# The second norm's features by 32x32 block transposes on VectorE and a round trip through memory

## The chip, the cores and the metric

One core of a Trainium2 chip runs the whole program. The metric is the device time of one execution in microseconds, as a median over runs. TensorE (PE in the profile) multiplies matrices and can transpose through the multiplier; PEld is its loading of stationary operands. VectorE is DVE, ScalarE is ACT, GpSimd is POOL, and SyncE (SP) here only issues transfers (DMAs).

## The reference

A transformer block with adaptive norms: attention on a modulated layer norm of `x`, then a gated MLP with a mixing over positions on a second modulated layer norm.

```python
x = A_x                                                     # 1 x 2048 x 448, float32
sa, ca, ga, sb, cb, gb = (silu(c) @ w_mod) in six parts of 448
h = layernorm(x) * (1 + ca) + sa
x = x + ga * attention(h, A_wqkv, A_wo)                     # 16 heads of 28
h = layernorm(x) * (1 + cb) + sb                            # the second norm
z = gelu(h @ B_w_in)                                        # 2048 x 1792
z1, z2 = z[..., :896], layernorm(z[..., 896:])
g = B_w_sp @ z2 + B_b_sp[:, None]                           # mixes the 2048 positions
out = x + gb * ((z1 * g) @ B_w_out)
```

## The kernel before

Everything is float32. Where precision matters, an operand is split in a high part (rounded to the matmul's reduced float32) and a low part, the difference, and a product is 11 matmuls over pairs of parts (`STEPS`): blocks 0 to 2 of the split hold the high parts of 384 features, blocks 3 to 5 their low parts, and block 6 the high and low parts of the last 64 features in its two halves. There is no scheduler: each engine's order is that in which the code is written (`manual_schedule`), and semaphores are put in where data or buffers demand it. One queue of SP carries nearly all transfers; a transfer that must wait holds up those behind it.

The stages in order: first norm and q, k, v; attention, head by head; then, from about 868 us, the part that this document is on; from 977 us the z2 product and its norm, the mixing over positions (a scheme with fewer products, given by tables), and the output product.

The 2048 rows are 16 tiles of 128, in four groups of four. In the part in question:

- `wo_mm(t)` is the output projection of attention for tile t, 11 matmuls into one PSUM bank; `wo_add(t)` adds it on DVE to the rows `x3[t]` and stores the sum to `x2_scr` for the end of the kernel. The last two matmuls of tiles 0 to 7 (`STEPS_Z`) wait for the last head and for `o_split`.
- `h2_stats(g)` takes mean and variance of a group's four tiles on DVE and 1/sqrt by a power on GpSimd (`rstd_of`). `h2_norm(g)` normalises the rows in place by two DVE instructions a tile: 448 columns, and the last 64 again beside them (they are wanted twice, for the halves of block 6).
- `h2_group(g)` calls `ln_transpose`: 16 TensorE transposes of 128x128 with the identity into four PSUM banks `tp`, so that features lie on partitions and 512 rows of the group along the free dimension. Then, for each of the four blocks, ACT applies scale and shift by feature into `hfull`, ACT copies that to the high part in `h2T[g]`, and DVE subtracts for the low part.
- `z1_unit(g, f)`, 28 of them, multiplies 128 columns of `w_in` with `h2T[g]` (11 matmuls), takes the gelu on ACT and stores the result to `z1_scr`. PSUM has seven banks in rotation here, so unit n reuses the bank of unit n - 7, once its gelu has read it.

`h2_group(0)` and `(1)` stand among the last projection tiles, `(2)` and `(3)` among the z1 units. The rows of `x` come in four loads, in which a group's row 128 t + p lies on partition p of tile t. `x2_load` at the end reads tile t back for the last addition. Buffers are reused by tags: `heapE` and `heapC` hold the `h2T` of groups 2 and 3, `x3` has three slots for the rows of groups 0 to 2 (group 3 lies in `heapC`) and later holds the buffer of the gelu outputs.

Of the kernel before, what the change touches and what calls it, by code (L numbers as in the profile page):

```python
# [8 lines left out]
F32 = mybir.dt.float32  # L9
F32R = mybir.dt.float32r  # L10
# [10 lines left out]
NG = 4  # L21
# [78 lines left out]
def tile_adaln_mha_gmlp(ctx, tc, x, wqkv, wo, w_in, w_spT, b_sp, w_out, cT, w_mod0, w_mod, out):  # L100
# [11 lines left out]
    x2_scr = scr.tile([S, D], F32, name="x2_scr")  # L112
    z1_scr = scr.tile([FH, S], F32, name="z1_scr")
    ws_scr = scr.tile([4 * len(W_SUMS), 128, 512], F32, name="ws_scr")
    wo2_scr = scr.tile([2, 7, 128, D], F32, name="wo2_scr")
    wl_scr = scr.tile([2 * len(W_SUMS), 128, 512], F32, name="wl_scr")

# [16 lines left out]
    def hview(heap, off, a, b):  # L134
        return heap[:, off : off + a * b].rearrange("p (a b) -> p a b", b=b)
# [913 lines left out]

    def h2_norm(g):  # L1050
        mv, rs, _ = mv3.pop(g)
        for tt in range(4):
            xt = x3[4 * g + tt]
            for o, i in ((xt[:, D:], xt[:, 384:D]), (xt[:, :D], xt[:, :D])):
                dve.tensor_scalar(
                    out=o, in0=i, scalar1=mv[:, tt, 0:1], scalar2=rs[:, tt : tt + 1], op0=ALU.subtract, op1=ALU.mult
                )

    raw_in = {}

# [53 lines left out]
        wo_mm(t, STEPS_MAIN)  # L1114
    o_split(3, 0, dve)
    o_split(3, 1, dve)
    for t in range(4):
        wo_mm(t, STEPS_Z)
        wo_add(t)
    o_split(3, 2, dve)  # L1120
    for t in range(4, 8):
        wo_mm(t, STEPS_Z)
        wo_add(t)
    o_split(3, 3, dve)
    h2_stats(0)
    h2_stats(1)
    h2_norm(0)
    heapF = dpool.tile([128, 4 * 896], F32R, name="heapF", tag="heapF")
    w2 = Halves(4, hview(heapD[2], 0, 4, 896), hview(heapF, 0, 4, 896))
    stg.close()  # L1130
    t3b = ph3.enter_context(tc.tile_pool(name="t3b", bufs=2))

    heaps = []

    def h2_group(g, after=None):
        if g >= 2:
            heaps.append(fh.tile([128, 4 * 896], F32R, name="heap", tag=("heapE", "heapC")[g - 2]))
            h2T.append(hview(heaps[-1], 0, 7, 512))
        xns = [x3.pop(4 * g + t) for t in range(4)]
        ln_transpose(xns, t3b, h2T[g], cols["cb"], cols["sb"], (act,) * 4, (dve,) * 4, None, after)  # L1140

    zbuf = []

# [18 lines left out]
    def last_tile(c):  # L1162
        if c == 2:
            wo_tile(15)
        h2_stats(2, ((0, 2, 1, 3).index(c),))

    h2_group(1, last_tile)
    h2_norm(2)
    h2_stats(3)
    win_load(0, t3)  # L1170
    win_load(1, t3b)
# [443 lines left out]
```

## Time and profile before

| | |
|---|---|
| median of 3 runs | 1377.51 us (1377.08 to 1378.38) |
| span of the profiled execution, first to last instruction | 1376.2 us |
| median less that span | 1.3 us |
| granted TensorE clock in the profile | 1.000 |
| stretch from the last attention sums to the z2 product | 868.3 to 977.1 us |
| TensorE transposes of the second norm | 64, from 892.6 to 932.1 us |

The profile lists the profiled execution's span and no other time of it; what lies around the span is therefore given by the difference to the median. The page gives each engine's busy time and share, the chain of work that ended last (followed back from the last instruction to whatever released each step), and groups of instructions by source line. The timeline gives instructions in order, runs of equal ones merged, with the engine's idle time before them and what ended it. A matmul's recorded duration contains its pipeline, so the cost of a run of matmuls is read from start to start.

### The profile page before, as it was taken

The page shows a single profiled execution, that of the slowest core. Times are in us where ns is not written, and L with a number is a line of the kernel's source. Part 1 is how long each engine was busy: PE and PEld are TensorE (multiplying, and loading weights), DVE is VectorE, ACT ScalarE, POOL GpSimd, SP SyncE. Part 2 cuts the span into 40 slices and gives each one's busy share as a digit, 9 for nine tenths or more (in the row PEclk, how much of TensorE's full clock was granted, in tenths as well). Part 3 has the DMA queues.
Part 4 walks back from the last instruction along what each step waited for, and adds up shares of the span by engine and source line. Part 5 has one row for each costly group of instructions (what it writes and reads, how often), then busy time and mean ns, then how long its engine had stood idle before and what let it go on. Part 6 is the DMA issues. An engine that isn't in the chain of part 4 may idle for free.

```text
span 1376.2 us, 20532 instructions
## 1 busy us (share of the span) xinstructions
PE 1370.9 (100%) x7098; PEld 974.6 (71%) x7098; DVE 1067.5 (78%) x1688; ACT 805.1 (59%) x1472; POOL 359.9 (26%) x367
## 2 busy tenths in 40 slices
PE   9999999999999999999999999999999999999998
PEld 8888655555555555555555554888898888888898
DVE  7898888888888888888888880673367777999752
ACT  6623666676667666766677779464324544555420
POOL 2134335243624264645640002200011000000000
PEclk9999999999999999999999999999999999999999
DMA  8465757777667667777773110535604665788552
GB/s 292 138 172 180 226 143 228 201 220 206 230 197 229 188 226 238 231 207 232 231 218 101 37 44 23 174 142 190 216 16 152 223 202 187 248 281 269 181 174 98
DMA packets 137075, 254.28 MB, mean 185 GB/s; under 512 B 21832, under 2 KB 37322, under 8 KB 134426
## 3 DMA queue, kind: packets, MB, share of 16 engines
q1 hardware_dynamic: 134254, 248.79, 57.7%
q10 hardware_dynamic: 2718, 4.19, 0.9%
q8 instruction: 56, 0.92, 0.3%
q14 instruction: 47, 0.39, 0.1%
HBM read 174.53 MB, written 73.59 MB: 180 GB/s over the span
## 4 chain that ended last, share of the span: by engine, by line
PE 97%; DVE 2%; issue 0%; DMA 0%; ACTq 0%; ACT 0%; POOL 0%; DVEq 0%
PE st_ps L741 19%; PE o_ps L756 17%; PE mt L709 17%; PE z_ps L1373 5%; PE acc L1441 5%; PE acc L1442 5%; PE acc L1440 5%; PE pq L404 5%; PE z_ps L1147 5%; PE pv L386 2%; PE y_ps L1508 2%; PE y_ps L1509 2%; PE y_ps L1507 2%; PE acc L1449 1%; PE acc L1450 1%; PE acc L1448 1%
## 5 line engine op out<-in xcount | busy, mean ns | idle before, releaser
L714 DVE TENSOR_REDUCE pm<-mt 128x1 f32<-128x512 f32 x1024 | 630.6, 680 | 86.1 <-PE mt L709 86.1
L745 ACT ACTIVATE P<-st_ps 128x512 f32<-128x512 f32 x1024 | 515.4, 626 | 202.6 <-PE st_ps L741 201.8
L741 PE MATMUL st_ps<-qst,kst 128*128 128x512 f32 x1024 | 406.3, 406 | 0.0
L709 PE MATMUL mt<-kst,qst 128*128 128x512 f32 x1024 | 402.8, 393 | 0.0
L741 PEld LDWEIGHTS st_ps<-qst,kst 128*128 128x128 f32 x1024 | 191.6, 188 | 140.8 <-issue 93.0
L756 PE MATMUL o_ps<-P,V 128*32 128x512 f32 x2048 | 246.3, 599 | 0.0
L709 PEld LDWEIGHTS mt<-kst,qst 128*128 128x128 f32 x1024 | 192.7, 188 | 31.5
L869 POOL TENSOR_TENSOR ws_raw<-ws_raw 128x512 f32<-128x512 f32 x112 | 143.6, 1288 | 177.7 <-DMA ws_raw<-in_w_spT_dram 110.5
L1357 ACT ACTIVATE heapB<-raw_sp 128x512 fp32r<-128x512 f32 x156 | 96.7, 630 | 98.4 <-PE acc L1442 68.3
L756 PEld LDWEIGHTS o_ps<-P,V 128*32 128x32 f32 x2048 | 53.7, 109 | 122.8 <-issue 117.4
L1442 PE MATMUL acc<-heapB,heapA 128*128 128x512 f32 x312 | 121.5, 390 | 0.0
L1440 PE MATMUL acc<-heapB,heapA 128*128 128x512 f32 x312 | 121.5, 390 | 0.0
L150 DVE TENSOR_TENSOR heapB<-raw_sp,heapB 128x512 fp32r<-128x512 f32 x112 | 74.6, 686 | 28.0 <-ACT heapB L1357 27.8
L1441 PE MATMUL acc<-heapB,heapA 128*128 128x512 f32 x222 | 86.6, 390 | 0.0
L1440 PEld LDWEIGHTS acc<-heapB,heapA 128*128 128x128 f32 x312 | 58.6, 188 | 12.2
L1442 PEld LDWEIGHTS acc<-heapB,heapA 128*128 128x128 f32 x312 | 58.6, 188 | 12.0
L404 PE MATMUL pq<-heapD,heapD 128*128 128x512 f32 x196 | 61.9, 390 | 0.0
L150 POOL TENSOR_TENSOR ws_raw<-ws_raw 128x512 fp32r<-128x512 f32 x44 | 56.6, 1287 | 3.5
L785 POOL TENSOR_TENSOR osb<-osb,rb 128x512 f32<-128x512 f32 x15 | 19.2, 1280 | 112.0 <-DMA rb<-r_scr 93.3
L1441 PEld LDWEIGHTS acc<-heapB,heapA 128*128 128x128 f32 x222 | 41.7, 188 | 8.9 <-DVE heapB L150 0.3
L1376 ACT ACTIVATE z<-z_ps 128x448 f32<-128x448 f32 x32 | 17.4, 544 | 47.7 <-PE z_ps L1373 47.7
L170 POOL TENSOR_TENSOR rsz<-rsz,mhalf 128x1 f32<-128x1 f32 x16 | 14.3, 891 | 118.1 <-DVE rsz L169 118.1
(218 smaller groups left out, 1652.8 us busy)
## 6 DMA issues: line engine op xcount, KB each, us to landing
ws_raw<-in_w_spT_dram SPq DMA_DIRECT2D x136, 256.0 KB
ws_scr<-ws_raw SPq DMA_DIRECT2D x112, 256.0 KB
ws_raw<-ws_scr SPq DMA_DIRECT2D x88, 256.0 KB
raw_sp<-ws_scr SPq DMA_DIRECT2D x88, 256.0 KB
raw_sp<-in_w_spT_dram SPq DMA_DIRECT2D x68, 256.0 KB
wl_scr<-ws_raw SPq DMA_DIRECT2D x44, 256.0 KB
kst<-qk_scr SPq DMA_DIRECT2D x45, 224.0 KB
qst<-qk_scr SPq DMA_DIRECT2D x45, 224.0 KB
```

The lines of the kernel that those rows point to most:

```text
L150: eng.tensor_tensor(out=dst, in0=a, in1=hi.bitcast(F32), op=ALU.subtract)
L404: pe.matmul(pq, wqk[:, b, m * 128 : (m + 1) * 128], hT[g][:, a, :], start=j == 0, stop=j == NST - 1)
L709: pe.matmul(mt, qst[h % 3][:, t * 128 : (t + 1) * 128], kst[h % 3][:, kb * 512 : (kb + 1) * 512], start=True, stop=True)
L714: dve.tensor_reduce(out=pms[h][:, t, kb : kb + 1], in_=mt, axis=AX.X, op=ALU.max)
L741: pe.matmul(st, kst[h % 3][:, kt * 128 : (kt + 1) * 128], qst[h % 3][:, qb * 512 : (qb + 1) * 512], start=True, stop=True)
L745: act.activation(p, st, AF.Exp, scale=SCALE)
L756: pe.matmul(otile[h][32 * qb : 32 * qb + 32, :], V[:, kt, h, :], ptiles.pop((u, qb)), start=kt == 0, stop=kt == NT - 1)
L869: pool.tensor_tensor(out=a, in0=a, in1=b, op=ALU.add if W_SUMS[v][2] > 0 else ALU.subtract)
L1357: act.activation(hi, raw[0], AF.Copy)
L1440: pe.matmul(o, zh[:, c], hi, start=p < 2 and kt == 0, stop=False, skip_group_check=p > 1)
L1441: pe.matmul(o, zh[:, c], lo, start=False, stop=False, skip_group_check=p > 1)
L1442: pe.matmul(o, zl[:, c], hi, start=False, stop=kt == 3, skip_group_check=p > 1)
```

## The change

The transposes of the second norm leave TensorE. The rows of a group are now normalised by ACT (one instruction a tile, with the scale 1/std and a bias `nb` = -mean/std that DVE computes in one small instruction). `h2_turn` lets DVE transpose all 32x32 blocks of a 128x448 tile in one instruction, four tiles a group, into a buffer `turn`, and four transfers store it, 32 partitions each, to `hs_scr[g]` in memory with features as rows. `h2_load` brings it back in five transfers into the low-part blocks of `h2T[g]` and both halves of block 6. `h2_group` then applies scale and shift from there on ACT, copies to the high parts, and subtracts into the low parts on DVE.

Block transposes leave the 32-row groups where they are, so the rows of `x` are laid out in another order when they are handed in: partition 32 a + i of tile t holds row 128 a + 32 t + i of its group. The program up to the second norm works on rows in that order unchanged; the stores put them in the true order, and `x2_load` gathers its 128 rows from four blocks of 32.

The code is written in another order, too: statistics and normalisation of group 0 move ahead of `wo_add` 4 to 7, those of group 1 ahead of `wo_add` 8 to 11, and `h2_turn` and `h2_load` of groups 2 and 3 stand among the z1 units.

```diff
     def h2_norm(g):
         mv, rs, _ = mv3.pop(g)
+        nb = t3.tile([128, 4], F32, name="nb3")
+        dve.scalar_tensor_tensor(out=nb, in0=mv[:, :, 0], scalar=-1.0, in1=rs, op0=ALU.mult, op1=ALU.mult)
         for tt in range(4):
-            xt = x3[4 * g + tt]
-            for o, i in ((xt[:, D:], xt[:, 384:D]), (xt[:, :D], xt[:, :D])):
-                dve.tensor_scalar(
-                    out=o, in0=i, scalar1=mv[:, tt, 0:1], scalar2=rs[:, tt : tt + 1], op0=ALU.subtract, op1=ALU.mult
-                )
+            xt = x3[4 * g + tt][:, :D]
+            act.activation(xt, xt, AF.Identity, scale=rs[:, tt : tt + 1], bias=nb[:, tt : tt + 1])
+
+    def h2_turn(g):
+        if g < 2:
+            blocks = fh.tile([128, 4 * 896], F32, name="turn", tag="heapE")
+        else:
+            blocks = t3.tile([128, 4, 512], F32, name="turn", tag="x3", bufs=3).rearrange("p a b -> p (a b)")
+        blocks = blocks[:, 0:1792].rearrange("p (b t i) -> p b t i", t=4, i=32)
+        for tt in range(4):
+            dve.transpose(blocks[:, :, tt, :], x3.pop(4 * g + tt)[:, :D])
+        for a in range(4):
+            sp.dma_start(
+                hs_scr[g].rearrange("(b j) n -> j b n", j=32)[:, :, a * 128 : (a + 1) * 128],
+                blocks[32 * a : 32 * a + 32].rearrange("p b t i -> p b (t i)"),
+            )
+
+    def h2_load(g):
+        if g >= 2:
+            heaps.append(fh.tile([128, 4 * 896], F32R, name="heap", tag=("heapE", "heapC")[g - 2]))
+            h2T.append(hview(heaps[-1], 0, 7, 512))
+        for c in (0, 2, 1):
+            sp.dma_start(h2T[g][:, 3 + c, :].bitcast(F32), hs_scr[g][c * 128 : (c + 1) * 128, :])
+        for r in (0, 64):
+            sp.dma_start(h2T[g][r : r + 64, 6, :].bitcast(F32), hs_scr[g][384:D, :])
...
-    def h2_group(g, after=None):
...
-        ln_transpose(xns, t3b, h2T[g], cols["cb"], cols["sb"], (act,) * 4, (dve,) * 4, None, after)
+    def h2_group(g):
+        for c in (0, 2, 1, 3):
+            f, hi = t3b.tile([128, 512], F32, name="hfull"), h2T[g][:, c if c < 3 else 6, :]
+            src = h2T[g][:, 3 + c, :].bitcast(F32)
+            act.activation(f, src, AF.Identity, scale=cols["cb"][:, c : c + 1], bias=cols["sb"][:, c : c + 1])
+            act.activation(hi, f, AF.Copy)
+            if c < 3:
+                sub(dve, h2T[g][:, 3 + c, :], f, hi)
+            else:
+                sub(dve, hi[64:128], f[64:128], hi[64:128])
...
     for t in range(8, 12):
         wo_tile(t)
-    h2_norm(1)
-    wo_mm(12, STEPS)
-    wo_add(12)
-    h2_group(0, lambda c: wo_tile(13) if c == 2 else None)
-    wo_tile(14)
...
-    h2_group(1, last_tile)
+    h2_turn(1)
+    h2_group(0)
+    h2_load(1)
+    for t in range(12, 16):
+        wo_tile(t)
+    h2_stats(2)
     h2_norm(2)
+    h2_group(1)
     h2_stats(3)
...
+            if g == 0 and f == 1:
+                h2_turn(2)
+                h2_load(2)
+                h2_norm(3)
             if g == 0 and f == 4:
+                h2_turn(3)
                 h2_group(2)
-                h2_norm(3)
+                h2_load(3)
...
-        sp.dma_start(x2t[t], x2_scr[t * 128 : (t + 1) * 128, :])
+        g, a = divmod(t, 4)
+        sp.dma_start(x2t[t], x2_scr.rearrange("(g t a i) d -> g a t i d", g=4, t=4, a=4)[g, a])
```

On TensorE, the end of the projection and the z1 units before (`tp` are the transposes' banks, `z_ps` those of z1):

```order
L831 MATMUL wo_ps<-heapD_91,heapD_90 128x448 x3
L1147 MATMUL z_ps<-heapB,heapA 128x512 x55
L179 MATMUL tp<-ident,x_10312 128x128 x16
L1147 MATMUL z_ps<-heapB,heapA 128x512 x55
L179 MATMUL tp<-ident,xl_10267 128x128 x16
L1147 MATMUL z_ps<-heapB,heapA 128x512 x44
L1147 MATMUL z_ps<-heap,heapA 128x512 x154
```

and now:

```order
L832 MATMUL wo_ps<-heapD_95,heapD_93 128x448 x2
L832 MATMUL wo_ps<-heapD_95,heapD_94 128x448 x3
L1177 MATMUL z_ps<-heapB,heapA 128x512 x154
L1177 MATMUL z_ps<-heap,heapA 128x512 x154
L1403 MATMUL z_ps<-heapD_95,heapB 128x448 x3
```

The four runs of 16 transposes are gone (two of them stood between projection tiles), and the 28 units of 11 matmuls follow each other directly.

On DVE, from the power of group 0 on (`x_10281` are the rows of group 0, `x_10283` of group 1, `x_10316` of group 2) it now reads:

```order
L170 TENSOR_SCALAR rs_10413<-mv_10412 128x4
L1054 SCALAR_TENSOR_TENSOR nb_10428<-mv_10412,rs_10413 128x4
L1035 TENSOR_TENSOR x_10283<-x_10283,wo_ps 128x448 x4
L1066 STREAM_TRANSPOSE turn<-x_10281 128x14x32 x4
L1044 BN_STATS st_10466<-x_10283 128x6
```

where before the statistics of group 1 followed those of group 0 and both stood behind all eight adds. The adds of tiles 4 to 7 now stand behind `nb`, which needs GpSimd's result.

On ACT, from the last block of group 1 on, before and now (`z1t` are the gelu outputs, `xl` the rows of group 3):

```order
L193 ACTIVATE heapB<-hfull 128x512
L1151 ACT_TABLE_LOAD
L1151 ACTIVATE z1t<-z_ps 128x512 x5
L186 ACTIVATE hfull<-tp,col_sb,col_cb 128x512
L193 ACTIVATE heap<-hfull 128x512
```

```order
L1166 ACTIVATE heapB<-hfull 128x512
L1181 ACT_TABLE_LOAD
L1181 ACTIVATE z1t<-z_ps 128x512 x2
L1057 ACTIVATE xl_10271<-xl_10271,nb_10733,rs_10667 128x448 x4
L1181 ACTIVATE z1t<-z_ps 128x512 x3
L1165 ACTIVATE hfull<-heap,col_sb,col_cb 128x512
L1166 ACTIVATE heap<-hfull 128x512
L1181 ACTIVATE z1t<-z_ps 128x512 x5
```

Group 3's normalisation now stands between the second and third gelu, and the work on group 2 (four pairs, of which the first is shown) stays between the fifth and the sixth, but waits for memory instead of TensorE.

More of the change, by code (lines that the diff above doesn't have):

```diff
@@ L1116, in tile_adaln_mha_gmlp @@
     o_split(3, 1, dve)
+    heapF = dpool.tile([128, 4 * 896], F32R, name="heapF", tag="heapF")
+    w2 = Halves(4, hview(heapD[2], 0, 4, 896), hview(heapF, 0, 4, 896))
     for t in range(4):
@@ L1120, in tile_adaln_mha_gmlp @@
     o_split(3, 2, dve)
+    o_split(3, 3, dve)
+    stg.close()
+    t3b = ph3.enter_context(tc.tile_pool(name="t3b", bufs=2))
+    h2_stats(0)
+    h2_norm(0)
     for t in range(4, 8):
@@ L1123, in tile_adaln_mha_gmlp @@
         wo_add(t)
-    o_split(3, 3, dve)
-    h2_stats(0)
+    h2_turn(0)
+    h2_load(0)
     h2_stats(1)
[L1127 to L1133, printed above, removed]
-    def h2_group(g, after=None):
[L1136 to L1139, printed above, removed]
-        ln_transpose(xns, t3b, h2T[g], cols["cb"], cols["sb"], (act,) * 4, (dve,) * 4, None, after)
+    h2_norm(1)
+    def h2_group(g):
[8 more added lines that the diff above has]
+                sub(dve, hi[64:128], f[64:128], hi[64:128])
     zbuf = []
```

8 lines of the change are left out of this document (3 added, 5 removed).

## The prediction

> **What bounds the kernel now.** I read the page first: busy shares and the chain that ended last.
>
> ```profile
> span 1376.2 us, 20532 instructions
> PE 1370.9 (100%) x7098; PEld 974.6 (71%) x7098; DVE 1067.5 (78%) x1688; ACT 805.1 (59%) x1472; POOL 359.9 (26%) x367
> PE 97%; DVE 2%; issue 0%; DMA 0%; ACTq 0%; ACT 0%; POOL 0%; DVEq 0%
> ```
>
> TensorE is the path almost everywhere, so a microsecond that leaves its queue, or a hole that opens in it, should move the end by a microsecond. Next, TensorE's timeline around the second norm (start, length, engine, line, operation):
>
> ```profile
> 868.30 24.48 PE L831 MATMUL wo_ps<-heapD,heapD 128*128 128x448 f32 x120
> 892.63 0.49 PE L179 MATMUL tp<-ident,x 128*128 128x128 f32 x3
> 893.40 1.71 PE L179 MATMUL tp<-ident,x 128*128 128x128 f32 x13 [0.29 <-DVE x L1055]
> 894.99 4.73 PE L831 MATMUL wo_ps<-heapD,heapD 128*128 128x448 f32 x22
> 899.56 2.09 PE L179 MATMUL tp<-ident,x 128*128 128x128 f32 x16
> 901.41 2.48 PE L831 MATMUL wo_ps<-heapD,heapD 128*128 128x448 f32 x11
> 903.73 12.66 PE L1147 MATMUL z_ps<-heapB,heapA 128*128 128x512 f32 x55
> 916.22 1.91 PE L179 MATMUL tp<-ident,x 128*128 128x128 f32 x16
> 917.88 12.74 PE L1147 MATMUL z_ps<-heapB,heapA 128*128 128x512 f32 x55
> 930.46 1.91 PE L179 MATMUL tp<-ident,xl 128*128 128x128 f32 x16
> 932.12 10.23 PE L1147 MATMUL z_ps<-heapB,heapA 128*128 128x512 f32 x44
> 942.20 35.07 PE L1147 MATMUL z_ps<-heap,heapA 128*128 128x512 f32 x154
> 977.10 0.77 PE L1373 MATMUL z_ps<-heapD,heapB 128*128 128x448 f32 x3
> ```
>
> It runs without a hole from the output projection through the 28 z1 units (11 matmuls each) to the z2 product at 977.10. A z1 unit takes (977.10 - 942.20) / 14 = 2.49, a projection tile of 11 matmuls 11 x 24.33 / 120 = 2.23. The later stages hang on TensorE, so I price the change by when that z2 product starts.
>
> **What is removed.** The four stretches of transposes, start to next start: 892.63 to 894.99 is 2.36 with its wait, then 1.85, 1.66, 1.66; together 7.5. Were all else hidden, the span would fall by 7.5. DVE's eight normalising instructions of a group leave too; DVE is not the path there now.
>
> **What is added is a chain over DVE, ACT and DMA**, for which these are the prices. First DVE (timeline, and two groups by shape, with busy time and mean ns of one):
>
> ```profile
> 879.06 2.21 DVE L1034 TENSOR_TENSOR x<-x,wo_ps 128x448 f32<-128x448 f32 x4
> 884.98 2.21 DVE L1043 BATCH_NORM_STATS2 st<-x 128x6 f32<-128x448 f32 x4
> 887.50 0.17 DVE L169 TENSOR_SCALAR rs<-mv 128x4 f32<-128x4 f32 x1
> 909.77 0.17 DVE L169 TENSOR_SCALAR rs<-mv 128x4 f32<-128x4 f32 x1
> 911.13 3.18 DVE L1055 TENSOR_SCALAR x<-x,mv,rs 128x64 f32<-128x64 f32 x8 [1.19 <-POOL rs L170]
> 918.43 0.69 DVE L150 TENSOR_TENSOR heap<-hfull,heap 128x512 fp32r<-128x512 f32 x1 [1.52 <-ACT heap L193]
> 871.90 1.03 DVE L1106 TENSOR_TENSOR osb<-osb,rb 128x512 f32<-128x512 f32 x1
> L1055 DVE TENSOR_SCALAR x<-x,mv,rs 128x448 f32<-128x448 f32 x12 | 6.2, 513 | 0.4
> L1386 DVE TENSOR_SCALAR z<-z,mvz,rsz 128x896 f32<-128x896 f32 x16 | 11.8, 739 | 0.4 <-POOL rsz L170 0.4
> ```
>
> Adds of four tiles 2.2; statistics of a group 887.67 - 884.98 = 2.7; the detour over GpSimd for the power 1.19, plus a small instruction for nb of 0.17: 1.36, in which DVE now stands still, with the next tiles' adds behind it (before, other groups' work filled most of such waits); a subtraction 0.7. No block transpose is in this trace. I take the time of the adds, 0.55 apart, 2.2 for four; ends: 0.51 (the one-source tensor_scalar of this size) and 1.03 (the slowest plain instruction on a tile here).
>
> ACT:
>
> ```profile
> 893.77 0.78 ACT L186 ACTIVATE hfull<-tp,col_sb,col_cb 128x512 f32<-128x512 f32 x1 [12.43 <-PE tp L179]
> 895.12 0.76 ACT L186 ACTIVATE hfull<-tp,col_sb,col_cb 128x512 f32<-128x512 f32 x1
> 907.84 1.28 ACT L1151 ACT_TABLE_LOAD   x1
> 909.14 1.09 ACT L1151 ACTIVATE z1t<-z_ps 128x512 f32<-128x512 f32 x2
> ```
>
> A scale-and-copy pair 1.35, so a group 5.4, as before but from SBUF; the four new normalisations about 0.62 each (a gelu is 0.55 from the next, a scaled 128x512 0.78 alone), 2.5 a group; table load 1.28, gelu 0.6.
>
> The round trip of a group, from the last block transpose to ACT's first read:
>
> ```profile
> 835.99 0.33 SPq L776 DMA_DIRECT2D r_scr<-rt  x1
> 837.40 0.59 SPq L782 DMA_DIRECT2D rb<-r_scr  x1
> 842.70 1.28 POOL L785 TENSOR_TENSOR osb<-osb,rb 128x512 f32<-128x512 f32 x1 [10.71 <-DMA rb<-r_scr]
> 865.87 1.34 SPq L1026 DMA_DIRECT2D x<-in_x_dram  x2
> 938.35 0.33 SPq L1177 DMA_DIRECT2D raw_out<-in_w_out_dram  x1
> 940.96 0.63 DVE L1181 TENSOR_TENSOR raw_out<-raw_out,bc_gb 128x448 f32<-128x448 f32 x1 [1.43 <-DMA raw_out<-in_w_out_dram]
> ```
>
> A store and then the issue of the load that waits for it: 1.41 (837.40 - 835.99), for 8 KB with a plain pattern; a three-level pattern like the new stores' takes 0.3 longer to issue (0.67 each for the two x loads). A load of 224 KB till its reader starts: 2.61. Between them lies the data, 4 x 224 KB = 917 KB from 32 partitions at a time. Rates, by windows (PE, PEld, DVE, ACT, POOL, clock, DMA share, GB/s); the first window moves 28 partitions at a time, the second 128:
>
> ```profile
> 874.10:878.10 4.00, 4.00 (x22) 3.71 (x21) 1.51 (x2) 1.58 (x3) 0.00 (x0) 1.00 0.49 114
> 879.50:889.00 9.50, 9.50 (x49) 8.82 (x48) 9.34 (x22) 1.79 (x3) 1.04 (x1) 1.00 1.03 365
> ```
>
> 114 GB/s at a share of 0.49 is 233 GB/s if full: 3.9 us. At 365 it would be 2.5, at half of that 5.0. I take 4.4, between the first and the last, because the narrow transfers are the nearest kind. Round trip: 1.41 + 0.3 + 4.4 + 2.61, less 0.1 for those 8 KB, 8.6; ends 6.7 and 9.2.
>
> The Trainium skill ("SBUF", section "Door 1: The DMA port swizzle") says that 32 neighbouring partitions reach only 8 of the 16 memory ports, which halves a transfer's rate. The narrow window above leans that way. By the rule alone (5.0) the round trip is 9.2 and the sum below ends 1.2 later; by the wide row alone (2.5) it is 6.7 and the sum ends 3.8 earlier.
>
> **The sum.** Nothing changes up to the second o_split (877). DVE: adds 0 to 3 from 879.06, two subtractions that stood elsewhere, statistics from 882.6 to 885.3, nb at 886.7, adds 4 to 7 till 888.9, block transposes till 891.1 (ACT's four normalisations run beside the adds). Round trip: group 0 can start on ACT at 899.7 (normalisation of group 1 has left ACT by 898). Group 5.4, last subtraction: 905.8. TensorE is out of projection tiles at 892.63 + 3 x 2.23 = 899.3 and can't finish z1 unit 0 before 906.2; before, it finished at 903.73 + 2.49 = 906.2 as well. So what two groups of transposes saved, the wait has eaten.
>
> From there the chain goes on without TensorE: adds 12 to 15 (queued on DVE behind the subtractions) 2.2, statistics 2.7, nb 1.36, normalisation of group 2 2.5, group 1 5.4 + 0.7: 920.7. Statistics 3 2.7, block transposes 2.2: 925.6. Round trip 8.6: 934.2. Group 2 5.4, gelu of z1 unit 5, which stands behind it on ACT, 0.6: 940.2. Unit 12 needs that unit's PSUM bank (seven in rotation), so it starts at 940.2, and 16 units of 2.49 are left: 980.1, against 977.10.
>
> TensorE alone would be earlier: unit 7 waits 0.7 for the first gelu (group 1 leaves ACT at 920.0, table load, gelu: 921.9), unit 9 some 2.0 for the normalisation of group 3, unit 12 the remaining 3.8. The other round trips (groups 1 and 3) have 8 us or more of z1 units over them.
>
> Hidden: the x2 loads of the last stage now gather four blocks. The one load here from four blocks, rb, took 842.70 - 837.40 = 5.3. They are issued two tiles ahead, and a tile takes 4.25:
>
> ```profile
> 1355.55 0.62 DVE L1512 TENSOR_TENSOR x2l<-x2l,y_ps 128x448 f32<-128x448 f32 x1 [3.64 <-PE y_ps L1509]
> 1359.80 0.62 DVE L1512 TENSOR_TENSOR x2l<-x2l,y_ps 128x448 f32<-128x448 f32 x1 [3.64 <-PE y_ps L1509]
> ```
>
> 8.5 covers 5.3; if the cover were gone, 3 us once. On SP's queue the stores of x2 tiles 8 to 15 and of z1 now stand behind loads that wait for the stores of their group; the z1 buffer has four slots, and the first gelu that needs such a store (unit 6) comes after the round trip anyway.
>
> Sum: +3.0 on a span of 1376.2; the median of the runs is 1377.51, 1.3 above the span, so 1380.5. A change of under 0.2% (2.8 us) is about what a measurement of this kernel can't tell from none.
>
> **Rivals.**
> *The round trip is shorter and the change is a wash.* It enters twice: each microsecond is 2 us of the end. From 6.7 (-0.8) to 8.4 (+2.6) the time is 1376.7 to 1380.1. For it: the stores may overlap better than the narrow window, which was not full. Against: that window is the only narrow one.
> *Faster.* One mechanism: the way through memory is short and the block transposes quick, so that unit 12 hardly waits. With 6.2 (stores bound only by their issue, 3 x 0.67, instead of 4.4 for data) and 0.3 a transpose, it starts at 940.2 - 2 x 2.4 - 8 x 0.25 = 933.4 and the end is 3.8 earlier than before: 1373.7. It decides below a round trip of 5.7, or of 6.7 with quick transposes. With every wait gone: 1370. For quick transposes: a one-source instruction grows from 513 to 739 ns for 448 elements more, 0.50 ns each, so half the adds' 0.55 can't be excluded. Against: the shortest row of the size is still 0.51. The Trainium skill ("VectorE: DVE Perf Modes", section "The perf-mode tier table") gives fp32 copies and tensor_scalar in SBUF twice the rate, which that slope bears out, but lists the stream shuffle at the single rate and doesn't list the transpose.
> *Slow block transposes.* At 1.03 each, two groups of them are on the chain: +3.8 more, 1384.3. Against: nothing shown needs it.
>
> **How the numbers follow.** Slower 0.48 (forecast 0.37, slow transposes 0.11), within 0.2% 0.42, faster 0.10. The forecast is the single most likely size, though it stands at the edge of what can be told. Range 1376.0 to 1384.5: from a short round trip (-0.8, and 0.7 for sums that round up) to slow transposes; the faster case and worse mixtures stay out.
>
> **What would show it.** After: no transposes by line 180 on PE; TensorE idle before its first z1 unit by about 4, before the sixth of group 1 (unit 12) by 2 to 4; the block transposes near 0.55; ACT waiting for the hs loads before groups 0 and 2; z2's first product near 980. Wrong if ACT's groups 0 and 2 start with the loads long landed, or if a wait arises after z1, where I expect none.

## The result, and the profile after

The changed kernel takes 1398.01 us (median of 4 runs, 1397.34 to 1400.88), the kernel before on the same chip 1377.3: a ratio of 1.015, 95% interval 1.0137 to 1.0162. It is 20.7 us slower, where 3.0 were forecast. The profiled execution is the slowest of the four: 1400.88 us, with a span of 1399.1 us.

The page: the transposes are gone from TensorE's count, and the span is longer with about as much busy time.

```profile
span 1399.1 us, 20444 instructions
PE 1373.8 (98%) x7034; PEld 970.0 (69%) x7034; DVE 1066.3 (76%) x1676; ACT 816.3 (58%) x1488; POOL 360.5 (26%) x367
```

TensorE's timeline, to be held against that of before (start, length, operation, count, and in brackets the idle time before it with what ended it; line 832 is the projection, 1177 z1, 1403 the z2 product). The stretch starts 0.7 earlier than before, at 867.59.

```profile
867.59 31.16 PE L832 MATMUL wo_ps<-heapD,heapD 128*128 128x448 f32 x153
900.67 0.49 PE L1177 MATMUL z_ps<-heapB,heapA 128*128 128x512 f32 x1 [1.92 <-ACT heapB L1166]
902.04 2.60 PE L1177 MATMUL z_ps<-heapB,heapA 128*128 128x512 f32 x8 [0.87 <-ACT heapB L1166]
905.51 15.71 PE L1177 MATMUL z_ps<-heapB,heapA 128*128 128x512 f32 x68 [0.87 <-DVE heapB L151]
921.88 5.29 PE L1177 MATMUL z_ps<-heapB,heapA 128*128 128x512 f32 x22 [0.66 <-ACT z1t L1181]
928.82 7.78 PE L1177 MATMUL z_ps<-heapB,heapA 128*128 128x512 f32 x33 [1.65 <-ACT z1t L1181]
942.23 8.00 PE L1177 MATMUL z_ps<-heapB,heapA 128*128 128x512 f32 x22 [5.63 <-ACT z1t L1181]
...
975.24 5.30 PE L1177 MATMUL z_ps<-heap,heapA 128*128 128x512 f32 x22 [1.13 <-ACT z1t L1181]
981.14 5.29 PE L1177 MATMUL z_ps<-heap,heapA 128*128 128x512 f32 x22 [0.61 <-ACT z1t L1181]
987.04 2.80 PE L1177 MATMUL z_ps<-heap,heapA 128*128 128x512 f32 x11 [0.61 <-ACT z1t L1181]
992.65 1.49 PE L1403 MATMUL z_ps<-heapD,heapB 128*128 128x448 f32 x3 [2.81 <-ACT z1t L1181]
...
998.82 1.17 PE L1403 MATMUL z_ps<-heapD,heapB 128*128 128x448 f32 x3 [2.23 <-ACT z1t L1181]
```

Down to unit 12 (942.23) this is nearly the forecast. What was not forecast stands below it: each second unit waits for a gelu, and the z2 product, which hung on nothing but TensorE before, waits twice more. That is the second sign of being wrong that the prediction named: a wait behind z1. From the first projection row the z2 product starts after 125.06 us (before: 977.10 - 868.30 = 108.80), and the mixing over positions, the stage behind it, after 203.3 (before 180.1).

Why the gelus are late is in ACT's and SP's timelines. First the blocked queue: group 3's stores (line 1068) and the loads that wait for them (1080, 1082) stand on SP's queue ahead of the z1 stores (1182), and the gelu of unit 9 waits 7.95 us for the store that frees its slot.

```profile
937.27 4.22 SPq L1068 DMA_DIRECT2D hs_scr<-turn  x4
944.67 1.29 SPq L1080 DMA_DIRECT2D heap<-hs_scr  x3
946.00 1.09 SPq L1082 DMA_DIRECT2D heap<-hs_scr  x2
947.14 11.36 SPq L1182 DMA_DIRECT2D z_scr<-z1t  x6
951.58 0.60 ACT L1181 ACTIVATE z1t<-z_ps 128x512 f32<-128x512 f32 x1 [7.95 <-DMA z_scr<-z1t]
```

Second, a loop. For every two units a part of `w_out` is loaded, scaled by DVE and copied by ACT (line 1208). The load is issued behind the z1 store of the even unit, the store waits for that unit's gelu, the copy waits for the load, and the next gelus stand behind the copy. One round after, from the gelu of unit 12 to the second copy (the row of stores covers those of units 11 and 12):

```profile
962.69 0.58 ACT L1181 ACTIVATE z1t<-z_ps 128x512 f32<-128x512 f32 x1
960.57 3.06 SPq L1182 DMA_DIRECT2D z_scr<-z1t  x2
963.68 0.42 SPq L1202 DMA_DIRECT2D raw_out<-in_w_out_dram  x1
967.05 0.62 DVE L1206 TENSOR_TENSOR raw_out<-raw_out,bc_gb 128x448 f32<-128x448 f32 x1 [1.81 <-DMA raw_out<-in_w_out_dram]
967.71 0.58 ACT L1208 ACTIVATE wout<-raw_out 128x448 fp32r<-128x448 f32 x1 [3.10 <-DVE raw_out L1206]
```

The first and the last of the seven copies, after and then before, and the group of them after and before (count, busy us, mean ns, then idle time before them with what ended it):

```profile
962.21 0.58 ACT L1208 ACTIVATE wout<-raw_out 128x448 fp32r<-128x448 f32 x1 [2.73 <-DVE raw_out L1206]
996.25 0.58 ACT L1208 ACTIVATE wout<-raw_out 128x448 fp32r<-128x448 f32 x1 [3.65 <-issue]
```
```profile
941.62 0.58 ACT L1183 ACTIVATE wout<-raw_out 128x448 fp32r<-128x448 f32 x1 [2.73 <-DVE raw_out L1181]
975.83 0.58 ACT L1183 ACTIVATE wout<-raw_out 128x448 fp32r<-128x448 f32 x1 [3.76 <-issue]
```
```profile
L1208 ACT ACTIVATE wout<-raw_out 128x448 fp32r<-128x448 f32 x7 | 4.0, 578 | 24.9 <-issue 19.1 <-DVE raw_out L1206 5.8
```
```profile
L1183 ACT ACTIVATE wout<-raw_out 128x448 fp32r<-128x448 f32 x7 | 4.0, 578 | 25.1 <-issue 14.9 <-DVE raw_out L1181 10.2
```

The seven copies take 34.0 us after (996.25 - 962.21) and took 34.2 before, 5.7 a round, against TensorE's 2 x 2.49 = 4.99 for two units. So the loop was there all along, slower than TensorE, with 25.1 us of idle ACT in it. Before, it ran from 941.62 to 975.83 and was through just ahead of the z2 product (977.10), so it cost nothing. Now ACT enters it 20.6 us later, can't catch up inside it, and TensorE stands at its end.

### The profile page after: what moved, and what is told of

It reads as the page before. It is cut to its first block, busy times and chain, and to the rows that moved or that the text cites. A ratio compares the mean times of both kernels' runs of the same rounds, so it can differ in the third digit from the quotient of the medians.

```text
span 1399.1 us, 20444 instructions
## 1 busy us (share of the span) xinstructions
PE 1373.8 (98%) x7034; PEld 970.0 (69%) x7034; DVE 1066.3 (76%) x1676; ACT 816.3 (58%) x1488; POOL 360.5 (26%) x367
## 5 line engine op out<-in xcount | busy, mean ns | idle before, releaser
L1177 PE MATMUL z_ps<-heapB,heapA 128*128 128x512 f32 x154 | 39.9, 416 | 11.6 <-ACT z1t L1181 7.9
```

## The experiments

Times of profiles are compared from the first projection row, since the programs are the same up to there and the executions reach it between 867.6 and 871.4 us. Ratios are to the kernel before on the same chip; the changed kernel's own is 1.015.

### The loop: which order makes it

**e4_wout.**
```diff
-        sp.dma_start(wouts[f][0], w_out[f * 128 : (f + 1) * 128, :])
+        pool.dma_start(wouts[f][0], w_out[f * 128 : (f + 1) * 128, :])
```


> The changed kernel with one edit: the seven loads of w_out go on POOL's queue, so that they don't stand behind z1 stores; these stay on SP's queue behind group 3's stores and loads. Theory B (a loop over two units, gelu, z1 store, w_out load behind it, DVE's product, ACT's copy, next gelu, holds ACT at 5.9 us for each two units and keeps it from catching up): ACT catches up after unit 14, the holes at z2's start go, and the time is 1386-1391 us. Rival (SP's blocked z1 store at unit 9 is all of it; ACT can't catch up in any case): 1395 us or more.

1387.22 us, ratio 1.0062 (1.0047 to 1.0077): the loop's theory. Group 3 still blocks the z1 stores, and unit 9's gelu still waits 7.2 us, but the copies wait less than half as long, and z1 runs through to the z2 product:

```profile
L1208 ACT ACTIVATE wout<-raw_out 128x448 fp32r<-128x448 f32 x7 | 4.0, 578 | 10.6 <-DVE raw_out L1206 7.3 <-DMA wo_scr<-wout 3.4
```
```profile
942.87 7.16 PE L1177 MATMUL z_ps<-heapB,heapA 128*128 128x512 f32 x22 [4.91 <-ACT z1t L1181]
949.87 7.64 PE L1177 MATMUL z_ps<-heap,heapA 128*128 128x512 f32 x33
958.09 27.74 PE L1177 MATMUL z_ps<-heap,heapA 128*128 128x512 f32 x121 [0.58 <-ACT z1t L1181]
```

Unit 12 starts as late as in the changed kernel; the 11 us are all gained behind it.

**e1_zstores.**
```diff
-        sp.dma_start(z1_scr[f * 128 : (f + 1) * 128, g * 512 : (g + 1) * 512], zt)
+        pool.dma_start(z1_scr[f * 128 : (f + 1) * 128, g * 512 : (g + 1) * 512], zt)
```


> The changed kernel with one edit: the 28 stores of z1 go on POOL's queue instead of SP's, so that none stands behind the stores and loads of the second norm. Theory A (the loss after unit 12 comes from SP's queue: ACT's 7.95 us wait for a z1 store, and the z1 stores and w_out loads that wait for one another there): that wait goes; unit 12 still waits some 5 us for group 2, the holes in z2 shrink to under 1 us each, and the time falls from 1398.0 to 1383-1389 us. Rival (the round trips and the norms on ACT themselves are the loss, whichever queue the z1 stores use): 1395 us or more.

1387.75 us, ratio 1.007 (1.0055 to 1.0085), within the forecast of theory A. But the same edit also takes the loads from behind the stores, so by itself it can't say whether the wait or the loop was the loss. It has a price, too: from the first of group 2's stores to its loads it took 9.38 us (929.89 to 939.27) instead of 7.59, and unit 12 waited 7.08 instead of 5.63.

**e5_wout_late.** Nothing changes its queue; the copy only comes later.
```diff
-            for fn, n in ((wout_load, 10), (wout_part, 11), (wout_store, 12)):
+            for fn, n in ((wout_load, 10), (wout_part, 13), (wout_store, 14)):
```


> The changed kernel with w_out's product, copy and subtraction three units behind their load instead of one (and their store four instead of two); all queues as in the changed kernel. Theory B (ACT stands behind the copy of a w_out part whose load is issued only two gelus earlier, once for each two units, and so can't catch up once it is behind): the load has landed when the copy's turn comes, ACT catches up, the holes at z2's start go, and the time is 1386-1390 us, as with the loads on another queue (1387.2). Rival (what mattered there was that SP's queue had less on it): 1395 us or more.

1388.12 us, ratio 1.0074 (1.0059 to 1.0089): the same gain without touching a queue. **c4_both** makes this edit and that of e1_zstores.

> The changed kernel with both cures of the loop: z1 stores on POOL's queue, and w_out's parts three units behind their load. If they cure the same thing (each alone gave 1387.7 and 1388.1), together they give 1385-1388 us, and what is left over the kernel before is the waits ahead of units 0, 7 to 12 and 14. Rival (each cures a loss of its own): 1377-1380 us.

1387.34 us, ratio 1.0066 (1.0052 to 1.008): three cures and two of them together give the same 10 to 11 us. That alone doesn't make them one cure, since with both TensorE has no wait left from unit 14 to the z2 product (951.47 to 986.37) that a second one could remove; what the three have in common is that they break the same loop.

**n3_same_queue** moves both kinds to POOL's queue (both edits above), where the load again stands behind the store.

> The changed kernel with z1 stores and w_out loads both on POOL's queue, so that SP's is free of them but each load stands again behind the store of the gelu ahead of it. If the order within a queue makes the loop (load behind store behind gelu behind copy behind load): the loop is back, 1394-1400 us, though each of the two moves alone gave 1387. Rival (it is the load on SP's queue that counts): 1387 us or less.

1405.01 us, ratio 1.0191 (1.0175 to 1.0206): the loop is back, and 5 us above the forecast, though SP's queue is empty of both. Its rounds took 6.8 us (first copy 959.96, last 1000.71); about half of what they took more lies between the load's issue and the copy, 4.1 to 4.3 us in the last four rounds against 3.6 to 3.7 in those of the changed kernel:

```profile
L1208 ACT ACTIVATE wout<-raw_out 128x448 fp32r<-128x448 f32 x7 | 4.0, 577 | 32.4 <-issue 24.4 <-DVE raw_out L1206 8.1
```

The order within a queue makes the loop, not the load on it.

### What makes ACT late

**e2_turn2.**
```diff
     h2_norm(2)
+    h2_turn(2)
+    h2_load(2)
     h2_group(1)
...
-                h2_turn(2)
-                h2_load(2)
                 h2_norm(3)
```


> The changed kernel with group 2's block transposes, stores and loads placed right behind its norm and ahead of group 1's normalisation instead of behind unit 1. Theory A (two separate losses: unit 12's wait for group 2, and the queue behind the stores and loads of group 3): unit 12's wait of 5.6 us and its stretch at half clock go, but the gelu of unit 9 still waits for a z1 store behind group 3's loads, and part of the gain is lost there: 1388-1393 us. Rival (all of the loss follows from the late group 2; once unit 12 is on time, ACT isn't behind either): 1380-1384 us. Second rival (ACT is the limit behind unit 12 whatever starts it): 1396 us or more.

1398.86 us, ratio 1.0144 (1.0129 to 1.0159), the second rival: ACT sets the time. Unit 12's wait shrank from 5.63 to 2.67, but the gelus now waited for their slots at two places (3.4 and 6.5 us), and all of the gain was lost in the loop: the copies began sooner (957.92), but took 36.0 us.

**e6_hs3_pool** puts group 3's stores and loads on POOL's queue.
```diff
-            sp.dma_start(
+            (pool if g == 3 else sp).dma_start(
...   # and the same for the five loads
```


> The changed kernel with group 3's stores and loads of the round trip on POOL's queue; z1 stores and w_out loads stay on SP's, so the loop over w_out is as in the changed kernel. Theory A+B (being late, by the 8 us wait at unit 9's gelu, and not catching up, by the loop, are both needed): the wait goes, but group 3's own loads still hold ACT until about 948 us, so that ACT is some 4 us less late and the time is 1391-1395 us. Rival (the loop alone sets the time, from the first w_out part on, however late ACT starts): 1397 us or more. Second rival (the blocked z1 store was the whole loss): 1386 us or less.

1397.02 us, ratio 1.0134 (1.0119 to 1.0149), at the lower edge of the first rival: the wait of 7.95 us shrank to 1.79, and that is worth 1 to 2 us, with intervals that overlap. (In the profiles the mixing starts 4.5 us sooner, counted from the first projection row, but the changed kernel's profiled execution is 2.9 above its median.) This was the first cause that the trace suggested, by its longest wait; with the loop in place it was little of the loss.

**c1_early** brings every step forward: group 2's norm ahead of group 0's normalisation, its round trip behind that, group 3's ahead of the z1 units, with z1 stores and w_out loads both on POOL's queue.
```diff
     h2_turn(1)
+    h2_load(1)
+    h2_stats(2)
+    h2_norm(2)
     h2_group(0)
-    h2_load(1)
+    h2_turn(2)
+    h2_load(2)
     for t in range(12, 16):
         wo_tile(t)
-    h2_stats(2)
-    h2_norm(2)
+    h2_stats(3)
+    h2_norm(3)
     h2_group(1)
-    h2_stats(3)
+    h2_turn(3)
+    h2_load(3)
...   # and out of the z1 units, where they stood
```


> The changed kernel with its causes taken away together: group 2's and group 3's statistics, norms, block transposes, stores and loads each placed one normalisation earlier (group 2's norm ahead of group 0's normalisation, group 3's behind the last w_o tile), and the z1 stores and w_out loads on POOL's queue. If the loss is late groups, the blocked queue and the w_out loop, nothing of it is left but the wait ahead of unit 0 (2.8 us) and a little of the round trips, against 7.5 us of transposes saved: 1372-1377 us, at or below the kernel before. Rival (VectorE and ACT, which now hold all of the second norm, become the bound in the w_o stretch and push z1 back as a whole): 1382 us or more.

1411.54 us, ratio 1.0242 (1.0225 to 1.0259): a miss by 35 us, and the slowest of all. Two reasons stand in its trace. ACT normalises the rows in place, so it must wait until their sums are stored; those stores now stand on SP's queue behind loads that wait for the round trip, and ACT, group 1 behind it, stands for 15.3 us:

```profile
924.00 2.29 SPq L1036 DMA_DIRECT2D x_scr<-xl  x4
927.69 2.72 ACT L1057 ACTIVATE xl<-xl,nb,rs 128x448 f32<-128x448 f32 x4 [15.31 <-DMA x_scr<-xl]
```

And its `w_out` loads stand behind the z1 stores on POOL's queue: the loop of n3_same_queue, with rounds of 6.9 us (first copy 965.65, last 1006.92).

**c3_early2** moves less, and has the two cures of c4_both.
```diff
     for t in range(12, 16):
-        wo_tile(t)
+        wo_mm(t, STEPS)
     h2_stats(2)
+    wo_add(12)
+    wo_add(13)
     h2_norm(2)
+    wo_add(14)
+    wo_add(15)
+    h2_stats(3)
+    h2_turn(2)
+    h2_load(2)
     h2_group(1)
-    h2_stats(3)
...
             if g == 0 and f == 1:
-                h2_turn(2)
-                h2_load(2)
                 h2_norm(3)
-            if g == 0 and f == 4:
                 h2_turn(3)
-                h2_group(2)
                 h2_load(3)
+            if g == 0 and f == 3:
+                h2_group(2)
```


> Both cures, and group 2 earlier without moving anything ahead of group 0's normalisation: group 2's statistics stand ahead of the sums of tiles 12 to 15 on VectorE, its norm, block transposes, stores and loads ahead of group 1's normalisation, group 3's norm and block transposes behind unit 1, group 2's normalisation behind unit 3. If what is left is the late group 2: its wait (5 us and its half clock) goes, the wait ahead of unit 0 (2.8 us) stays, and 7.5 us of transposes are saved: 1373-1377 us, below the kernel before. Rival (ACT's norms and normalisations, 8.4 us a group, delay the gelus by as much elsewhere): 1380 us or more.

1376.26 us against 1377.72, ratio 0.9989 (0.998 to 0.9998): within the forecast, just below the kernel before, by less than can well be told, and 22 us faster than the changed kernel with the same work. Of the waits ahead of z1 units, that of the first unit is nearly all that is left:

```profile
901.05 0.57 PE L1177 MATMUL z_ps<-heapB,heapA 128*128 128x512 f32 x1 [2.04 <-ACT heapB L1166]
902.42 30.20 PE L1177 MATMUL z_ps<-heapB,heapA 128*128 128x512 f32 x120 [0.80 <-ACT heapB L1166]
932.96 7.79 PE L1177 MATMUL z_ps<-heapB,heapA 128*128 128x512 f32 x33 [0.34 <-ACT z1t L1181]
940.59 35.07 PE L1177 MATMUL z_ps<-heap,heapA 128*128 128x512 f32 x154
```

**n1_early_loop** and **n2_early_late** have this order with neither cure, and with the late copy alone.

> The order of c3_early2 (group 2 and 3 earlier) without either cure of the loop: z1 stores, w_out loads and the round trips all on SP's queue, w_out's parts one unit behind their load. If the loop costs only what ACT is late when it enters it (its rounds take 5.7 to 5.9 us for two units, TensorE's 5.0, so seven rounds lose some 5 us more, against seven banks of slack): group 3's loads still hold up the z1 stores, ACT enters it some 6 us earlier than in the changed kernel, and the time is 1383-1390 us. Rival (the loop is harmless once group 2 is early): 1375-1378 us, as c3_early2. Second rival (the loop sets the time however early ACT enters it, as in e2_turn2 and e6_hs3_pool): 1395 us or more.

> The order of c3_early2 with w_out's parts three units behind their load, but the z1 stores on SP's queue behind group 3's stores and loads. If the blocked z1 stores cost nothing by themselves (e5_wout_late and c4_both differ by 0.8 us): 1375-1379 us, as c3_early2. Rival (with group 2 early, the blocked stores are the next bound on ACT): 1382 us or more.

n1: 1394.25 us, ratio 1.0114 (1.0099 to 1.0129), 4 us above its forecast and just short of the second rival. n2: 1383.99 us, ratio 1.0043 (1.003 to 1.0055), 5 us above its forecast, and the rival: with group 2 early, the blocked z1 stores are the next bound (a gelu waits 8.7 us for its slot, TensorE 4.7 us for that gelu). In n1 the copies ran from 955.85 to 989.87, once more 34.0 us. So wherever load stands behind store on SP's queue, the last copy comes 33 to 36 us behind the first, and the mixing starts 73 to 76 us behind the last (each row in the time of its own profile, in which the first projection row stands between 867.6 and 868.7):

| | first copy | last copy | between | mixing starts |
|---|---|---|---|---|
| before | 941.62 | 975.83 | 34.2 | 1048.44 |
| changed | 962.21 | 996.25 | 34.0 | 1070.92 |
| n1_early_loop | 955.85 | 989.87 | 34.0 | 1063.22 |
| e6_hs3_pool | 958.64 | 991.96 | 33.3 | 1067.54 |
| e2_turn2 | 957.92 | 993.89 | 36.0 | 1069.40 |
| e4_wout (loop cured) | 960.57 | 982.57 | 22.0 | 1057.00 |
| c3_early2 (loop cured) | 951.26 | 973.33 | 22.1 | 1046.83 |

### TensorE's clock behind the holes

Windows of the changed kernel across the hole ahead of unit 12 (busy times of PE, PEld, DVE, ACT, POOL, then the granted clock, DMA share and GB/s): half clock for 6.8 us.

```profile
940.00:942.00 2.00, 0.00 (x0) 0.00 (x0) 0.97 (x2) 1.97 (x4) 0.00 (x0) 0.80 1.01 298
942.00:944.00 2.00, 1.77 (x4) 1.49 (x5) 0.41 (x1) 1.64 (x4) 0.00 (x0) 0.50 0.81 222
944.00:946.00 2.00, 2.00 (x6) 1.52 (x6) 0.00 (x0) 0.00 (x0) 0.00 (x0) 0.50 0.24 36
946.00:948.00 2.00, 2.00 (x7) 1.52 (x6) 0.00 (x0) 0.00 (x0) 0.00 (x0) 0.50 0.90 331
948.00:950.00 2.00, 2.00 (x10) 1.66 (x9) 0.00 (x0) 0.00 (x0) 0.00 (x0) 0.99 0.92 319
```

**e3_fill** keeps TensorE busy there.
```diff
+        for a, b in STEPS * FILL.get((g, f), 0):   # FILL = {(1, 4): 2, (3, 6): 1}
+            pe.matmul(ps_t, w1[:, b, ...], h2T[g][:, a, :], start=True, stop=True)
```


> The changed kernel with 33 matmuls added whose results are thrown away: 22 ahead of unit 11's own and 11 ahead of unit 27's, so that TensorE is busy in the holes ahead of unit 12 and of z2 (7 us more work at full clock). Theory C (the half clock behind these holes is a loss of its own): unit 12 and the first tiles of z2 run at full clock, and the time falls by 3 to 5 us, to 1393-1395 us, with more work. Rival (ACT sets the pace there, and the half clock only fills time in which TensorE would wait for a bank): the time stays at 1397-1399 us, and the waits for ACT's gelu grow by what the clock gives.

1401.51 us, ratio 1.0174 (1.0156 to 1.0192), some 3 us slower than the changed kernel, though the intervals overlap: theory C fails, and the rival's range is missed as well. Units 11 to 13 did run at full clock, from 940.39 without a wait, but TensorE then waited 1.84 and 1.07 for gelus in later rounds, where it had waited 0.50 and 0.20. Ahead of z2 the hole only moved: the first product waited 0.25, the second half tile 3.66, and behind that the clock was halved for 6.83 us, so of the two holes only that ahead of unit 12 was tested.

**c5_filled** is c3_early2 with the same idea at unit 0.
```diff
+        for _ in range(12 if (g, f) == (0, 0) else 0):
+            pe.matmul(ps_t, w1[:, 0, 0:128], w1[:, 0, 0:512], start=True, stop=True)
```


> The kernel of c3_early2 with 12 matmuls of w_in's parts by themselves, thrown away, ahead of unit 0's own, so that TensorE is busy in the hole of 2.0 us in which it waits for the first normalised columns. In c3_early2's profile the granted clock was 0.50 from 902 to 908 us behind that hole, in the changed kernel's profile it stayed 1.00 behind a hole of the same length. If the half clock costs time where nothing else waits (theory C, which failed behind unit 12, where ACT set the pace): unit 0 to 2 run at full clock and up to 3.4 us go, 1373-1375 us. Rival (another wait takes them up again, as behind unit 12): 1376 us or more, with new waits for the gelus of unit 7 onwards.

1379.9 us, ratio 1.0008 (0.9999 to 1.0017), 2.6 us slower than c3_early2 by the ratios, not faster: the rival. The clock stayed at 1.00 from 900 to 914 us, units 0 to 10 were done sooner, and the time came back as a wait of 2.69 us for the gelu that frees unit 11's bank, with half clock behind it:

```profile
906.53 25.68 PE L1179 MATMUL z_ps<-heapB,heapA 128*128 128x512 f32 x112 [0.86 <-DVE heapB L151]
934.90 9.37 PE L1179 MATMUL z_ps<-heapB,heapA 128*128 128x512 f32 x33 [2.69 <-ACT z1t L1183]
```

From the first projection row the z2 product starts 2.7 us later than in c3_early2 (110.36 against 107.64). Of this 1.1 arose ahead of unit 11, since ACT's waits for group 2's loads came to 2.8 us instead of 1.6, and 1.6 in the half clock behind it. Why those loads came later the runs don't show. But in c3_early2, too, unit 11 started when a gelu was done, so a full clock ahead of it had nothing to win.

So in both places the half clock filled time in which TensorE would have waited for ACT.

### The two halves of the change by themselves

**r2_dve_norm**: block transposes and round trip, norms by VectorE.
```diff
-        nb = t3.tile([128, 4], F32, name="nb3")
-        dve.scalar_tensor_tensor(out=nb, in0=mv[:, :, 0], scalar=-1.0, in1=rs, op0=ALU.mult, op1=ALU.mult)
...
-            act.activation(xt, xt, AF.Identity, scale=rs[:, tt : tt + 1], bias=nb[:, tt : tt + 1])
+            dve.tensor_scalar(
+                out=xt, in0=xt, scalar1=mv[:, tt, 0:1], scalar2=rs[:, tt : tt + 1], op0=ALU.subtract, op1=ALU.mult
+            )
```


> The changed kernel with its other half undone: the second norm by VectorE again (one subtract-and-multiply of 128x448 a tile), block transposes and round trip as changed. ACT is freed of four times 2.7 us. If the loop over w_out sets the time behind unit 12 whatever comes before it: 1392-1398 us. Rival (ACT's 10.9 us of norms are what put it behind, so that without them it never falls into the loop): 1388 us or less.

1398.93 us, ratio 1.0151 (1.0135 to 1.0166), 0.9 above the forecast: without ACT's 10.9 us of norms the loss is the same. The copies ran from 961.71 to 995.99, as in the changed kernel. The norms cost time on VectorE instead (unit 0 starts 35.3 us behind the first projection row, in the changed kernel 33.1), so the run shows that ACT's norms aren't what the loss hangs on, not that they are free.

**b1_actnorm**: the kernel before with norms by ACT, TensorE's transposes kept.
```diff
+        nb = t3.tile([128, 4], F32, name="nb3")
+        dve.scalar_tensor_tensor(out=nb, in0=mv[:, :, 0], scalar=-1.0, in1=rs, op0=ALU.mult, op1=ALU.mult)
...
-                dve.tensor_scalar(
-                    out=o, in0=i, scalar1=mv[:, tt, 0:1], scalar2=rs[:, tt : tt + 1], op0=ALU.subtract, op1=ALU.mult
-                )
+                act.activation(o, i, AF.Identity, scale=rs[:, tt : tt + 1], bias=nb[:, tt : tt + 1])
```


> The kernel before with one part of the change: the second norm by ACT (scale and bias for each row) instead of VectorE; TensorE's transposes, their order and the padding columns stay, so ACT has eight activations a group, some 3.5 us. If that part costs nothing by itself (ACT has 3 us and more free a group there, and the banks hold seven units): 1377-1380 us. Rival (ACT's time goes straight into the chain from the norms to the transposes and the gelus): 4 groups of some 3.5 us less what VectorE took, 1383 us or more.

1383.08 us, ratio 1.0039 (1.0023 to 1.0055): the rival by its number. TensorE's stretches of transposes grew, by waits for ACT (the first from 2.36 to 3.80 us, 892.63 to 896.43), and the z2 product started at 980.73 instead of 977.10. This run meets the loop as well, with TensorE's transposes still in place: the copies ran from 947.71 to 982.32, once more 34.6 us, the last of them behind the start of the z2 product, which then waited 0.80 us for a gelu.

## Why the prediction was wrong, point by point

- *What is removed, 7.5 us*: right as work. c3_early2 shows what the best order tried kept of it: with waits of 3.2 us (2.04 + 0.80 + 0.34) and a half clock of 6.8 us behind the first of them, it gained 1 to 2.
- *The prices of the chain*: right. The block transposes of a group took 2.22 (2.2 taken), so the rival of slow ones is out; a group on ACT took 5.5 to 5.7 (5.4), the table load 1.28. ACT's normalisations took 2.72 a group (2.5 taken).
- *Round trip 8.6*: 8.95 for group 0, from the end of its last block transpose (890.19) to ACT's first read, inside the ends; 10.39 for group 2 (925.49 to 935.88), above the upper end of 9.2. The two issue rows between them show where:

```profile
887.97 2.22 DVE L1066 STREAM_TRANSPOSE turn<-x 128x448 f32<-128x448 f32 x4
890.21 3.02 SPq L1068 DMA_DIRECT2D hs_scr<-turn  x4
896.53 1.29 SPq L1080 DMA_DIRECT2D heapB<-hs_scr  x3
899.14 0.81 ACT L1165 ACTIVATE hfull<-heapB,col_sb,col_cb 128x512 f32<-128x512 f32 x1 [2.34 <-DMA heapB<-hs_scr]
```
```profile
923.27 2.22 DVE L1066 STREAM_TRANSPOSE turn<-x 128x448 f32<-128x448 f32 x4
925.51 3.01 SPq L1068 DMA_DIRECT2D hs_scr<-turn  x4
933.10 1.29 SPq L1080 DMA_DIRECT2D heap<-hs_scr  x3
935.88 0.81 ACT L1165 ACTIVATE hfull<-heap,col_sb,col_cb 128x512 f32<-128x512 f32 x1 [6.15 <-DMA heap<-hs_scr]
```

  From the first store's issue to the load's issue it was 6.32 and 7.59, where 6.0 were taken; from there to ACT 2.6 and 2.8, as taken (2.61). The stores were the mis-sized part; why the second four took 1.3 longer was not tried (in e4_wout they took 6.35). By the port rule of the Trainium skill ("SBUF — State Buffer", section "Door 1: The DMA port swizzle") the round trip was estimated at 9.2: group 0 came within 0.25 of that and group 2 lay 1.2 above it, and no run here moved the same data over more partitions.
- *Unit 12 starts at 940.2*: 942.23, and unit 7 waited 0.66 (0.7 forecast), unit 9 1.65 (2.0), unit 12 5.63 (3.8). The rival of a short way through memory is out.
- *"16 units of 2.49 are left: 980.1"*: the step that failed. It took 50.4 us (942.23 to 992.65) instead of 39.9, and the z2 stage behind it, taken over from before without a term of its own, 78.27 instead of 71.34. The profiled execution took 1400.88, 20.4 over the forecast: 2.0 by unit 12, 10.5 and 6.9 by these two terms, 0.4 behind the start of the mixing, and 0.5 because its time lay 1.8 above its span, where the prediction took 1.3, the distance of a median from the span of one execution. (The median of the changed kernel is 2.9 lower; in which stage the other executions were shorter isn't on record.) Of the 10.5, 2.8 are the half clock in units 12 and 13 (7.83 us from start to start instead of 4.99), and the rest waits for gelus. Of the 6.9, 2.2 are the second wait, some 3.3 an estimate for two stretches of half clock (992.41 to 995.82 and 999.23 to 1002.64, in which about 6.6 us of work ran at half speed), and 1.3 the slower half tiles of the last section. The sum counted from unit 12 on as if TensorE had no one to wait for. It had found the one gelu that releases unit 12, and not asked what the gelus behind it wait for.
- *"The z1 buffer has four slots, and the first gelu that needs such a store (unit 6) comes after the round trip anyway"*: failed for group 3, whose stores and loads blocked the queue until 947 and the gelu of unit 9 until 951.58. The step looked at one round trip and not at the next. Its price alone was small, though (e6_hs3_pool), until the loop and the late group 2 were gone (n2_early_late against c3_early2: 7.7 us).
- *The x2 loads at the end, hidden*: right. From the start of the mixing to the end of the span it was 327.8 before (1376.2 - 1048.44) and 328.2 after.
- The rows that would have told were in the profile before: the copies' 25.1 us of idle time, 10.2 of them put down to DVE's `raw_out` and 14.9 to nothing that the profile shows ("issue"), in rounds of 5.7 us. The prediction quoted one such load for its 2.61 us and didn't read the group. As ACT wasn't the bound, the idle time seemed free; its slack was seven banks, and the change used them up.

By the runs, what the changed kernel loses against c3_early2, some 22 us, splits in two of 11 us each. From 1376.3 (c3_early2) to 1387.3 (c4_both) it is groups 2 and 3 being late, and from there to 1398.0 the loop. (The kernel before took 1377.7 beside the first two, 1377.3 beside the third.) They aren't independent: curing the loop with late groups gives 11, curing the lateness within the loop 4 (n1_early_loop), both 22.

## What to carry to other kernels

When a change makes an engine late, look for the loops that it then runs behind: a round that is slower than the bottleneck's, hidden by buffers, costs nothing until the buffers are used up, and its length stands in the old profile as idle time of an engine that isn't the bound. A load put behind a store on one queue inherits everything that the store waits for; another queue or a later use mends it, and moving both to the other queue doesn't. The longest wait in a trace isn't the cause by its length: one of 8 us was worth 1 to 2 here, seven of 3.5 us were worth 11.

## What the hardware showed beyond that

- In the profiles of this case the granted clock, once halved, stayed so for 3.41, 6.83, 10.24 or 13.65 us between 880 and 1012 us, and for no length between these. In the changed kernel it fell at 941.21, 992.41 and 999.23, which are 15 and 2 times 3.41 apart. The Trainium skill ("TensorE: Matmul & The Clock Gate", section "What's actually happening") has a free-running window of 3413 ns and asks for one idle window; the length agrees, and so does the fixed grid. But the window needn't be all idle: in c3_early2 the clock fell at 901.36 (worked out from 0.84 in the window of 900 to 902 us) after 3.41 us of which TensorE's rows leave 2.04 empty. A hole of 1.92 at the same place in the changed kernel left it at 1.00; there the grid (941.21 less 12 windows is 900.25) cuts the hole in two parts, 1.50 and 0.42.

```profile
900.00:902.00 2.00, 0.57 (x1) 0.19 (x1) 0.69 (x1) 1.94 (x4) 0.00 (x0) 0.84 0.96 328
902.00:904.00 2.00, 1.58 (x4) 1.29 (x5) 0.92 (x2) 1.97 (x4) 0.00 (x0) 0.50 1.00 347
```

- Half tiles of the z2 product follow each other every 2.23 us before and in most runs, but every 2.27 in the changed kernel, e2_turn2, e6_hs3_pool and n3_same_queue, at a granted clock of 1.00 (from 1010 to 1040 us, before from 985 to 1020). Over 32 of them that is 1.3 us. What sets it stays open.
- The changed kernel and e1_zstores are equal up to z1, but their executions reached the projection 3.8 us apart (867.59 and 871.39), and 2.7 of that arose in the first 15 us.
